# Fourier-domain channel mixing and MLP on one core: some DRAM stores issued from ScalarE's queue, with a reordered start of the second sequence

## The chip, the cores and the metric

The kernel runs on one core of a Trainium2 chip. The core has TensorE (PE, matrix multiply), VectorE (DVE), ScalarE (ACT), GpSimd (POOL) and SyncE (SP); in this kernel SP does nothing but issue DMA transfers. Each engine takes its own instructions in order. The metric is the device time of one execution in microseconds (us); less is better.

## The reference

The input x is 8 sequences of 3136 rows with 256 channels, in f32.

```
X  = rfft(x, axis=1)
Yr = Xr @ w_r - Xi @ w_i + b_r ;  Yi = Xr @ w_i + Xi @ w_r + b_i
Y  = soft-threshold(Yr, Yi, 0.01)
x1 = irfft(Y, n=3136)
u  = x1 + real(fft(fft(x1, axis=1), axis=2))
un = (u - mean(u)) / sqrt(var(u) + 1e-6)          # over the 256 channels
out = u + relu(un @ w_ch1) @ w_ch2                # 256 -> 1024 -> 256
```

The MLP weights arrive as 64-bit floats.

## The kernel before, in words

Each sequence goes through a chain of stages, each written as a Python generator. The transform over 3136 rows is split as 64 x 49.

- `p1` (for the first sequence, number 0, `p1_first`): loads x in chunks (`xf`), multiplies by the 64-point table (matmul L337 for sequence 0, L397 for sequence 1), copies the result out of PSUM into `ev` (ScalarE for even chunks, VectorE for odd ones), and stores `ev` into a DRAM scratch `a`. For sequence 0 that scratch lies in three parts: `a0` (frequencies 0 to 7), `a8` (8 to 15) and `ad` (16 to 31). The stores to `a0` go out first (L355). The stores to `a8` are gathered in a list `next8` (11), all others in a list `rest` (13). L362 issues `next8` and the first four of `rest` (15 in all), L367 the other nine.
- `p2_f2`: in four quarters q of eight frequencies each, two halves s per quarter, loads `af` (from `a`) and the table `tff` (L448, L450), and does the 49-point transform (matmul L468, 32 per quarter). The results are split into a high and a low part (`Xh`, `Xl`, `Xsh`, `Xsl`). The buffers `af` and `tff` are rings of three.
- `p2_w`: the complex channel product with the tables `wr`, `ws`, `wd`, three matmuls for one product (L154 to L156, tile `g_w`), then bias and soft threshold on VectorE (L534 to L537) into `Y`.
- `p2_mix`: the channel-axis transform of `Y`, put together in the tile `mq` on ScalarE, VectorE and GpSimd (L598 to L614), and stored to the DRAM scratch `md` (L619 to L633): ten stores for q = 0, six for each other quarter. `mq` is a ring of two.
- `p2_yt`, `p2_g2`: transposes of `Y` and the inverse 49-point transform, stored to `bd` (L696).
- `p3_norm`, `p3_tr`, `p3_mlp1`, `p3_mlp2`: the inverse 64-point transform (from `bd`, L720), the sum with `md` (loaded as `mt`, L740 and L742) into `ut` (L751), the statistics, and the two MLP products (tiles `h`, `o`).
- `weights`: loads the 64-bit MLP weights in eight pieces (`raw_w`, issued at L285; w1 in the buffers `W2` and `W3`, w2 in `Xh` and `Xl`, one buffer each) and splits each into a high and a low f32 part with six operations on VectorE (L179 to L189), two on ScalarE and two on GpSimd.

All f32 products but the simplest are three matmuls of split parts (`mm3`). The results in PSUM of all stages up to the MLP share four buffers (tag `g`).

The order of work is set in two steps. A heap takes the next step of the generator with the earliest due time (in units of T, the time slot of one sequence), which fixes the order in which instructions are written down; `after(...)` holds a generator back until another has passed a point. Then, when the program is built, each engine's instructions are ordered by readiness in a planned timeline, so that an instruction that is ready sooner can be put ahead of one written down earlier. `tc.issue_after(i)` keeps instructions of the same engine behind instruction i. Once built, the order on each engine is fixed. `behind(key, ...)` is a load on SP held behind an earlier load (key 3: the second `af` load of q = 1).

Before the change every DMA of the kernel is issued from SP (`st_eng = nc.sync`).

Of the kernel before, what the change touches and what calls it, by code (L numbers as in the profile page):

```python
# [132 lines left out]
def spectral_block(ctx: ExitStack, tc: tile.TileContext, x, w_ri, b_ri, w1, w2,  # L133
# [159 lines left out]
    def n2_rows(t, n0, n):  # L293

        return t[n0:n0 + n].rearrange("n c u d -> (c u) n d")
# [9 lines left out]
    def p1_first():  # L305


        a0 = dr.tile([N2, 2, 8, D], F32, tag="a0", bufs=1, name="a0")
        a8 = dr.tile([N2, 2, 8, D], F32, tag="a8", bufs=1, name="a8")
        ad = dr.tile([N2, 2, U - 16, D], F32, tag="ad0", bufs=1, name="ad0")  # L310
        ad1 = dr.tile([N2, 2, U, D], F32, tag="ad", bufs=4, name="ad1")
        a_dram[0] = lambda u: (a0, u) if u < 8 else (a8, u - 8) if u < 16 else (ad, u - 16)
        a_dram[1] = lambda u: (ad1, u)

        loads = [("xf", 2, 1)] * 2 + [("ut", UTB, 1)] * 2 + [("Y", 2, 3)] * 2 + [("Xh", 1, 2)]
        stores = [("uth", 2, 2), ("utl", 2, 2)] * 2 + [("W0", 1, 4)]
        slots = []
        for tag, bufs, z in loads:
            slots += [(tag, bufs, z, i) for i in range(z)]
        outs = []  # L320
        for tag, bufs, z in stores:
            outs += [(tag, bufs, z, i) for i in range(z)]
        slots.append(("Xl", 1, 1, 0))
        outs.append(("ev", 2, 1, 0))
        next8, rest = [], []
        todo = chunks + [(NM - 1, 1)]
        for ci, (m, n) in enumerate(todo):
            yield T * ci / len(todo)
            w = n * D
            tag, bufs, z, i = slots[ci]  # L330
            if i == 0:
                xf = sb.tile([128, z * 512], F32, tag=tag, bufs=bufs, name="xf")
                nn = z * 2 if n == 2 else 1
                for r, src in enumerate(x_rows(0, m, nn)):
                    af_ld["x"] = nc.sync.dma_start(out=xf[r * 64:r * 64 + 64, :nn * D], in_=src).ins
            g = gtile("g_f1")
            te.matmul(g[:, :w], fwd_0, xf[:, i * 512:i * 512 + w], start=True, stop=True)  # L337
            tag, bufs, z, i = outs[ci]
            if i == 0:
                ev = sb.tile([128, z * 512], F32, tag=tag, bufs=bufs, name="ev")  # L340
            (va.tensor_copy if ci % 2 else sc.copy)(ev[:, i * 512:i * 512 + w], g[:, :w])
            if i == z - 1:
                mb = m - 2 * i
                nn = m + n - mb
                for r in range(2):
                    v = ev[:, :nn * D].rearrange("p (n d) -> p n d", d=D)
                    if n == 1:
                        if r:

                            st_eng.dma_start(out=ad1[m:m + 1, :, 0:8].rearrange("n c u d -> c u (n d)"), in_=ev[16:32, :D])  # L350
                            rest.append((ad1[m:m + 1, :, 8:16].rearrange("n c u d -> c u (n d)"), ev[48:64, :D]))
                            rest.append((ad1[m:m + 1, :, 16:].rearrange("n c u d -> c u (n d)"), ev[96:128, :D]))
                            continue
                    n2 = NM * r + mb
                    st_eng.dma_start(out=n2_rows(a0, n2, nn), in_=v[r * 16:r * 16 + 16])  # L355
                    next8.append((n2_rows(a8, n2, nn), v[32 + r * 16:48 + r * 16]))
                    rest.append((n2_rows(ad, n2, nn), v[64 + r * 32:96 + r * 32]))
        done.add(("a0", 0))
        yield from after(("af", 1))
        for o, i in next8 + rest[:4]:  # L360
            with tc.issue_after(af_ld[1]):
                af_ld["rest"] = st_eng.dma_start(out=o, in_=i).ins  # L362
        done.add(("a8", 0))
        yield from after(("af", 3))
        for o, i in rest[4:]:
            with tc.issue_after(af_ld[3]):
                st_eng.dma_start(out=o, in_=i)  # L367
        done.add(("a", 0))

    def p1(b):  # L370
# [18 lines left out]
        for ci, (m, n) in enumerate(todo):  # L389
            yield T * (t0 + width * (ci - 1) / len(todo))  # L390
            load(ci)
            yield T * (t0 + width * ci / len(todo))
            w = n * D
            xf = xfs.pop(ci)
            g = gtile("g_f1")
            if b == 1:
                te.matmul(g[:, :w], fwd_f, xf[:, :w], start=True, stop=True)  # L397
            else:
                xh = sb.tile([128, 512], F32R, tag="xh", bufs=1, name="xh")
                xl = sb.tile([128, 512], F32R, tag="xl", bufs=1, name="xl")  # L400
                sc.copy(xh[:, :w], xf[:, :w])  # L401
                lo_g(xl[:, :w], xf[:, :w], xh[:, :w])
                mm3(g[:, :w], *K["fwd"], xh[:, :w], xl[:, :w])
            ev = sb.tile([128, 512], F32, tag="ev", bufs=2, name="ev")
            (va.tensor_copy if ci % 2 else sc.copy)(ev[:, :w], g[:, :w])
            for r in range(2):
                ad, n2 = (a_dram[b + r](0)[0], m) if n == 1 else (a_dram[b](0)[0], NM * r + m)
                st_eng.dma_start(out=n2_rows(ad, n2, n),
                                 in_=ev[r * 64:r * 64 + 64, :w].rearrange("p (n d) -> p n d", d=D))
        done.add(("a", b))  # L410

# [3 lines left out]
        t0 = T * (1.0, START1)[b] if b < 2 else T * (b + 2 - LEAD)  # L415
        return t0 + step * q, step, f2w, w0, ww, w0 + ww
    xt, yt_, tabs = {}, {}, {}
    w_mm, last_mm = {}, [None]

    def behind_w(b, on):  # L420

# [12 lines left out]
    def p2_f2(b):  # L434


        for q in range(4):
            base, STEP, F2W, W0, WW, M0 = clock2(b, q)
            u0 = 8 * q
            yield base  # L440
            yield from after((("a0", "a8")[q] if b == 0 and q < 2 else "a", b))
            xt[b, q] = Xh, Xl, Xsh, Xsl = x_tiles(b, q)
            afs, tfs = [], []
            for s in range(2):
                af = sb.tile([98, 4 * D], F32, tag="af", bufs=3, name="af")
                ad, u = a_dram[b](u0 + 4 * s)
                with tc.issue_after(af_ld["rest"]) if b == 0 and q == 1 else nullcontext():
                    ld = nc.sync.dma_start(out=af, in_=ad[:, :, u:u + 4].rearrange("n c u d -> (n c) (u d)"))  # L448
                tff = sb.tile([98, 4, 100], F32, tag="tff", bufs=3, name="tff")
                nc.sync.dma_start(out=tff, in_=c_tf[:, u0 + 4 * s:u0 + 4 * s + 4, :])  # L450
                afs.append(af)
                tfs.append(tff)
                if b == 0:
                    af_ld[2 * q + s] = ld.ins
                    done.add(("af", 2 * q + s))
            for ui in range(4):
# [6 lines left out]
                for s in range(2):  # L463
                    yield base + STEP * F2W * (ui / 4 + s / 8)
                    for k in range(2):
                        o = gv[:, k, :, s * S:s * S + S]
                        with behind_w(0, b == 0 and q == 1 and ui == 0):
                            te.matmul(o, afs[s][:, ui * D + k * 128:ui * D + k * 128 + 128], tfs[s][:, ui].rearrange("p (c j) -> p c j", c=2),  # L468
                                      start=True, stop=True)
                def put(f, outs, *ins):  # L470

                    both = len(outs[0]) == 1
# [70 lines left out]
    def p2_mix(b):  # L543
# [6 lines left out]
        def rows(d, first, nj, n):  # L550

            return d[first:first + 64 * nj].rearrange("(j k) d -> j k d", k=64)[:, 0:n]
# [3 lines left out]
        for q in range(4):  # L556
# [58 lines left out]
            mr = mq.rearrange("p a u h e -> p a (u h e)")  # L615
            mp, mm = (mq[:, i].rearrange("p u h e -> p u (h e)") for i in range(2))

            if q:
                st_eng.dma_start(out=rows2(u0, 24), in_=mr[0:24])  # L619
                st_eng.dma_start(out=rows2(u0 + 64 * 24, 1), in_=mr[24:25])  # L620
                st_eng.dma_start(out=rows2(61 - u0, 24), in_=mr[75:99])
            else:
                st_eng.dma_start(out=rows(mpd, 0, 25, 4), in_=mp[0:25])
                st_eng.dma_start(out=rows(mmd, 0, 25, 3), in_=mm[0:25, 1:4])
                st_eng.dma_start(out=rows(mpd, 61, 24, 3), in_=mp[75:99, 0:3])
                st_eng.dma_start(out=rows(mmd, 60, 24, 3), in_=mm[75:99, 0:3])

                st_eng.dma_start(out=rows(mmd, 63, 24, 1), in_=mm[1:25, 0:1])
                st_eng.dma_start(out=rows(mpd, 32, 24, 1), in_=mp[75:99, 3:4])
                st_eng.dma_start(out=rows(mmd, 31, 25, 1), in_=mm[75:100, 3:4])  # L630
            st_eng.dma_start(out=rows2(u0 + 4, 24), in_=mr[50:74])
            st_eng.dma_start(out=rows2(u0 + 4 + 64 * 24, 1), in_=mr[74:75])
            st_eng.dma_start(out=rows2(57 - u0, 24), in_=mr[25:49])  # L633
        done.add(("m", b))

    yhl = {}
# [278 lines left out]
```

## Time and profile before

| | us |
|---|---|
| three runs | 1932.55, 1924.45, 1930.68 |
| median | 1930.68 |
| profiled execution: its own time | 1925.76 |
| profiled execution: span, first to last instruction | 1923.5 |
| PE busy in the span | 1844.0 (96%) |
| DVE, ACT, POOL busy | 1259.7 (65%), 851.1 (44%), 701.5 (36%) |

The page of the profile cuts the span into 40 slices of 48 us. In the first four PE is busy 5, 7, 8 and 6 tenths, from then on nine tenths or more. The start, until the MLP of the first sequence runs, is thus where PE stands idle, and there the change lies. The span is the time between the first and the last instruction; the time of the execution has 2.3 us more around it.

### The profile page before, as it was taken

The page shows a single profiled execution, that of the slowest core. Times are in us where ns is not written, and L with a number is a line of the kernel's source. Part 1 is how long each engine was busy: PE and PEld are TensorE (multiplying, and loading weights), DVE is VectorE, ACT ScalarE, POOL GpSimd, SP SyncE. Part 2 cuts the span into 40 slices and gives each one's busy share as a digit, 9 for nine tenths or more (in the row PEclk, how much of TensorE's full clock was granted, in tenths as well). Part 3 has the DMA queues.
Part 4 walks back from the last instruction along what each step waited for, and adds up shares of the span by engine and source line. Part 5 has one row for each costly group of instructions (what it writes and reads, how often), then busy time and mean ns, then how long its engine had stood idle before and what let it go on. Part 6 is the DMA issues. An engine that isn't in the chain of part 4 may idle for free.

```text
span 1923.5 us, 34657 instructions
## 1 busy us (share of the span) xinstructions
PE 1844.0 (96%) x12123; PEld 1695.2 (88%) x12123; DVE 1259.7 (65%) x2726; ACT 851.1 (44%) x1892; POOL 701.5 (36%) x1093
## 2 busy tenths in 40 slices
PE   5786999999999999999999999999999999999999
PEld 3665999989999999989999999998999999998899
DVE  2886767767666766767666666765766776665443
ACT  2555545444544444444444544434454443433322
POOL 0455544333434334344323444323443332323110
PEclk7897999999999999999999999999999999999999
DMA  7666644354443545244443543435533343223110
GB/s 205 180 202 179 175 134 115 102 156 137 122 114 112 142 120 150 84 123 138 119 143 93 155 130 105 127 94 150 145 95 109 102 115 89 69 80 115 56 40 26
DMA packets 163715, 233.02 MB, mean 121 GB/s; under 512 B 27662, under 2 KB 107606, under 8 KB 163542
## 3 DMA queue, kind: packets, MB, share of 16 engines
q1 hardware_dynamic: 163542, 230.82, 42.5%
q8 instruction: 96, 1.57, 0.3%
q14 instruction: 77, 0.63, 0.1%
HBM read 127.95 MB, written 102.76 MB: 120 GB/s over the span
## 4 chain that ended last, share of the span: by engine, by line
PE 82%; DMA 6%; DVE 5%; SPq 3%; issue 1%; ACT 1%; POOL 1%; DVEq 0%; POOLq 0%; ACTq 0%
PE o L155 9%; PE o L154 9%; PE o L156 8%; PE h L154 8%; PE h L156 8%; PE h L155 8%; PE g_f L468 5%; PE g_w L154 3%; PE g_w L156 3%; PE g_w L155 3%; PE g_yt L663 2%; PE g_g L154 2%; PE g_g L155 2%; PE g_g L156 2%; PE g_ut L785 2%; DMA md<-mq 2%
## 5 line engine op out<-in xcount | busy, mean ns | idle before, releaser
L807 DVE SCALAR_TENSOR_TENSOR hl<-h,hh 128x512 fp32r<-128x512 f32 (+1 forms) x416 | 272.9, 656 | 332.7 <-ACT hh L806 330.8
L806 ACT ACTIVATE hh<-h 128x512 fp32r<-128x512 f32 (+1 forms) x416 | 238.5, 573 | 475.1 <-PE h L156 438.4
L155 PE MATMUL o<-w2h,hl 128*128 128x256 f32 x1568 | 429.0, 284 | 3.1 <-DVE hl L807 2.9
L156 PE MATMUL o<-w2h,hh 128*128 128x256 f32 x1568 | 422.7, 279 | 0.0
L154 PE MATMUL o<-w2l,hh 128*128 128x256 f32 x1568 | 391.3, 284 | 0.0
L154 PE MATMUL h<-utl,w1h 128*128 128x512 f32 (+1 forms) x832 | 323.9, 389 | 0.0
L156 PE MATMUL h<-uth,w1h 128*128 128x512 f32 (+1 forms) x832 | 317.7, 382 | 0.0
L155 PE MATMUL h<-uth,w1l 128*128 128x512 f32 (+1 forms) x832 | 317.5, 382 | 0.0
L155 PEld LDWEIGHTS o<-w2h,hl 128*128 128x128 f32 x1568 | 296.8, 189 | 9.3 <-DVE hl L807 4.2
L156 PEld LDWEIGHTS o<-w2h,hh 128*128 128x128 f32 x1568 | 296.4, 189 | 3.4
L154 PEld LDWEIGHTS o<-w2l,hh 128*128 128x128 f32 x1568 | 283.7, 189 | 12.5
L151 POOL TENSOR_TENSOR bl<-bf,bh 128x512 fp32r<-128x512 f32 x104 | 130.2, 1252 | 286.9 <-ACT bh L745 284.3
L156 PEld LDWEIGHTS h<-uth,w1h 128*128 128x128 f32 x832 | 156.3, 188 | 23.9
L151 POOL TENSOR_TENSOR xl<-xf,xh 128x512 fp32r<-128x512 f32 (+1 forms) x75 | 98.4, 1311 | 213.0 <-ACT xh L401 207.0
L154 PEld LDWEIGHTS h<-utl,w1h 128*128 128x128 f32 x832 | 156.6, 188 | 14.2 <-DVE hl L807 0.3
L155 PEld LDWEIGHTS h<-uth,w1l 128*128 128x128 f32 x832 | 156.7, 188 | 13.5
L468 PEld LDWEIGHTS g_f<-tff,af 98*128 98x128 f32 x1024 | 145.2, 199 | 24.3 <-issue 11.2
L468 PE MATMUL g_f<-tff,af 98*128 98x100 f32 x1024 | 151.9, 278 | 14.8 <-DMA tff<-c_tf 14.2
L151 POOL TENSOR_TENSOR Xl<-xx,Xh 128x400 fp32r<-128x400 f32 (+1 forms) x96 | 99.8, 1041 | 77.3 <-ACT Xh L482 39.7
L751 DVE TENSOR_TENSOR ut<-g_g,mt 128x512 f32<-128x512 f32 x104 | 68.2, 656 | 87.2 <-PE g_g L156 43.1
L151 POOL TENSOR_TENSOR Xsl<-xs,Xsh 128x200 fp32r<-128x200 f32 x120 | 75.5, 630 | 133.8 <-ACT Xsh L482 123.3
L760 POOL TENSOR_SCALAR vv<-ag 128x2 f32<-128x2 f32 x104 | 27.1, 260 | 208.8 <-DVE ag L757 185.2
(162 smaller groups left out, 3795.4 us busy)
## 6 DMA issues: line engine op xcount, KB each, us to landing
bd<-bev SPq DMA_DIRECT2D x128, 196.0 KB
bf<-bd SPq DMA_DIRECT2D x184, 128.0 KB
out_dram<-ut SPq DMA_DIRECT2D x92, 256.0 KB
af<-ad SPq DMA_DIRECT2D x60, 392.0 KB
xf<-in_x SPq DMA_DIRECT2D x176, 128.0 KB
ad<-ev SPq DMA_DIRECT2D x176, 128.0 KB
md<-mq SPq DMA_DIRECT2D x112, 192.0 KB
mt<-md SPq DMA_DIRECT2D x416, 32.0 KB
```

The lines of the kernel that those rows point to most:

```text
L151: gp.tensor_sub(out_, full, hi.bitcast(F32))
L154: te.matmul(o, lh, rl, start=start, stop=False)
L155: te.matmul(o, ll, rh, start=False, stop=False)
L156: return te.matmul(o, lh, rh, start=False, stop=stop)
L468: te.matmul(o, afs[s][:, ui * D + k * 128:ui * D + k * 128 + 128], tfs[s][:, ui].rearrange("p (c j) -> p c j", c=2), start=True, stop=True)
L663: te.transpose(gt[:100, (v * 2 + o) * 128:(v * 2 + o + 1) * 128], y[:, o, place].rearrange("p c j -> p (c j)"), ident)
L751: va.tensor_add(ut[:, :n], g[:, :w].rearrange("p (n d) -> p n d", d=D), mt[:, :n])
L760: gp.tensor_scalar(vv[:, :n], ag[:, :n, 1:2], 1.0, EPS, op0=ALU.mult, op1=ALU.add)
L785: te.transpose(gv[:, k, j * 128:(j + 1) * 128], ut[:, j, k * 128:(k + 1) * 128], ident)
L806: sc.activation(hh[:, :w], h[:, :w], AF.Relu)
L807: va.scalar_tensor_tensor(hl[:, :w], h[:, :w], 0.0, hh[:, :w].bitcast(F32), op0=ALU.max, op1=ALU.subtract)
```

## The change

Five things are changed, all of them in the first two sequences:

1. Of the 15 stores at L362 every second one (7), and of the nine at L367 every second one (4), is issued from ScalarE's queue (`nc.scalar`), without `issue_after`. SP keeps 8 and 5.
2. The first-stage matmuls of sequence 1 are written down only once `p2_f2` has written the second pair of frequencies of q = 1 of sequence 0, and the first of them is kept behind that matmul on PE (`f2_mm[0, 1, 1]`).
3. The first-stage stores of sequence 1 (L408, 24 of them) go out from ScalarE's queue for even chunks (12).
4. For sequence 0, q = 2, the loads of `af` and `tff` are due 0.1 T earlier and go into other buffers: one slot of the `mq` ring for both halves of `af`, the two slots of `eo` for `tff`.
5. All 28 `mq` stores of sequence 0 are issued from ScalarE's queue.

```diff
-        for o, i in next8 + rest[:4]:
+        for n, (o, i) in enumerate(next8 + rest[:4]):
+            if n % 2:
+                nc.scalar.dma_start(out=o, in_=i)
+                continue
             with tc.issue_after(af_ld[1]):
                 af_ld["rest"] = st_eng.dma_start(out=o, in_=i).ins
...
-        for o, i in rest[4:]:
+        for n, (o, i) in enumerate(rest[4:]):
+            if n % 2:
+                nc.scalar.dma_start(out=o, in_=i)
+                continue
             with tc.issue_after(af_ld[3]):
                 st_eng.dma_start(out=o, in_=i)
...
+            while b == 1 and (0, 1, 1) not in f2_mm:
+                yield now[0] + 10
...
             if b == 1:
-                te.matmul(g[:, :w], fwd_f, xf[:, :w], start=True, stop=True)
+                with tc.issue_after(f2_mm[0, 1, 1]) if ci == 0 else nullcontext():
+                    te.matmul(g[:, :w], fwd_f, xf[:, :w], start=True, stop=True)
...
-                st_eng.dma_start(out=n2_rows(ad, n2, n),
+                (nc.scalar if b == 1 and ci % 2 == 0 else st_eng).dma_start(out=n2_rows(ad, n2, n),
...
-    w_mm, last_mm = {}, [None]
+    w_mm, last_mm, f2_mm = {}, [None], {}
...
-            yield base
+            yield base - (0.1 * T if b == 0 and q == 2 else 0)
...
-                af = sb.tile([98, 4 * D], F32, tag="af", bufs=3, name="af")
+                roomy = b == 0 and q == 2
+                if roomy:
+                    if s == 0:
+                        wide = sb.tile([98, 8 * D], F32, tag="mq", bufs=2, name="af")
+                    af = wide[:, s * 4 * D:(s + 1) * 4 * D]
+                else:
+                    af = sb.tile([98, 4 * D], F32, tag="af", bufs=3, name="af")
...
-                tff = sb.tile([98, 4, 100], F32, tag="tff", bufs=3, name="tff")
+                tff = sb.tile([98, 4, 100], F32, tag="eo" if roomy else "tff", bufs=2 if roomy else 3, name="tff")
...
-                            te.matmul(o, afs[s][:, ui * D + k * 128:ui * D + k * 128 + 128], tfs[s][:, ui].rearrange("p (c j) -> p c j", c=2),
-                                      start=True, stop=True)
+                            f2_mm[b, q, ui] = te.matmul(o, afs[s][:, ui * D + k * 128:ui * D + k * 128 + 128], tfs[s][:, ui].rearrange("p (c j) -> p c j", c=2),
+                                      start=True, stop=True).ins
...
+            mix_eng = nc.scalar if b == 0 else st_eng
             if q:
-                st_eng.dma_start(out=rows2(u0, 24), in_=mr[0:24])
+                mix_eng.dma_start(out=rows2(u0, 24), in_=mr[0:24])
...
```

The other nine kinds of `mq` store are changed in the same way as the last one shown.

## Rows read from the trace of the kernel before

**Rows 1.** Busy time by stretch: the stretch in us from the span's start, its length, then the busy time of each engine with its instructions, the granted clock of TensorE as a share of full speed, the busy share of the 16 DMA engines, and GB/s.

```profile
26.00:46.00 20.00, 11.44 (x44) 10.74 (x44) 3.61 (x9) 5.30 (x15) 4.32 (x6) 0.51 0.87 232
46.00:62.00 16.00, 8.92 (x39) 7.81 (x40) 11.73 (x19) 4.73 (x9) 6.21 (x5) 0.68 0.79 230
62.00:85.00 23.00, 17.41 (x87) 12.75 (x85) 22.32 (x41) 13.13 (x38) 15.69 (x22) 0.93 0.53 147
85.00:117.00 32.00, 30.36 (x182) 25.88 (x180) 19.91 (x43) 19.67 (x53) 14.26 (x18) 1.00 0.66 188
117.00:157.00 40.00, 29.25 (x131) 22.85 (x131) 38.72 (x63) 20.05 (x46) 23.95 (x19) 0.83 0.70 210
157.00:200.00 43.00, 31.29 (x149) 26.53 (x149) 24.62 (x51) 21.47 (x48) 23.75 (x32) 0.80 0.61 168
...
200.00:400.00 200.00, 197.58 (x1342) 183.13 (x1340) 144.76 (x308) 98.72 (x223) 87.81 (x123) 1.00 0.46 128
```

**Rows 2.** Instructions of PE in order of time: start, duration, line, what; in brackets the idle time before and what ended it.

```profile
30.91 7.12 PE L468 MATMUL g_f<-tff,af 98*128 98x100 f32 x32 [9.64 <-DMA tff<-c_tf]
...
45.14 0.48 PE L156 MATMUL g_w<-Xh,wsh 128*128 128x400 f32 x1
53.08 2.04 PE L397 MATMUL g_f<-xf,fwd_f 128*128 128x512 f32 x2 [7.46 <-DMA xf<-in_x]
...
71.74 0.66 PE L468 MATMUL g_f<-tff,af 98*128 98x100 f32 x4 [3.15 <-DMA tff<-c_tf]
...
90.25 1.03 PE L468 MATMUL g_f<-tff,af 98*128 98x100 f32 x8
...
99.21 0.66 PE L468 MATMUL g_f<-tff,af 98*128 98x100 f32 x4 [1.40 <-DMA tff<-c_tf]
...
160.15 1.03 PE L468 MATMUL g_f<-tff,af 98*128 98x100 f32 x8
```

**Rows 3.** The chain of waits that ended last, from 36 to 64 us, in order of time: start, duration, what.

```profile
38.23 5.68 DMA tff<-c_tf
...
46.10 3.97 DMA raw_w<-in_w
...
50.10 0.43 DVE cv_w_ut L183
```

**Rows 4.** DMA issues of SP in order of time: start, duration of all together, line, what, count.

```profile
1.19 6.94 SPq L335 DMA_DIRECT2D xf<-in_x  x11
9.09 0.81 SPq L355 DMA_DIRECT2D a<-ev  x2
...
26.86 7.64 SPq L362 DMA_DIRECT2D a<-ev  x11
34.54 2.04 SPq L362 DMA_DIRECT2D ad<-ev  x4
...
38.66 7.38 SPq L367 DMA_DIRECT2D ad<-ev  x9
46.10 0.87 SPq L285 DMA_DIRECT2D raw_w<-in_w  x2
```

**Rows 5.** The DMA queue from 0 to 26 us: packets, MB, and the time that the packets took as a share of the 16 engines' time; under it two groups of store issues up to 70 us, with their count and the size of each.

```profile
q1 hardware_dynamic: 3655, 4.95, 74.6%
...
ad<-ev SPq DMA_DIRECT2D x14, 128.0 KB
...
a<-ev SPq DMA_DIRECT2D x16, 64.0 KB
```

**Rows 6.** The chain of waits around 119 us and from 165 to 185 us.

```profile
117.74 0.60 DVE ev L405
...
119.04 0.62 SPq L408
...
119.76 3.92 DMA raw_w<-in_w
...
168.03 0.17 DVE mq L613
...
169.47 0.60 SPq L408
...
170.84 0.49 SPq L619
...
173.58 3.88 DMA md<-mq
177.48 0.33 SPq L740
...
179.70 1.65 DMA mt<-md
```

**Rows 7.** Store issues on SP: line, what, count, and the shortest, median and longest duration in ns, with the first and last start (tile `mq` from 80 to 200 us; line L408 up to 220 us).

```profile
L408 SPq DMA_DIRECT2D ad<-ev x38: 574/620/1522, 55.8 to 219.4; - x38
...
L631 SPq DMA_DIRECT2D md<-mq x4: 305/374/378, 104.8 to 172.5; - x4
L632 SPq DMA_DIRECT2D md<-mq x4: 592/616/634, 105.1 to 172.9; - x4
...
L619 SPq DMA_DIRECT2D md<-mq x3: 303/317/491, 127.1 to 170.8; - x3
```

**Rows 8.** What SP's DMA queue waited for up to 220 us, of these stores alone: line and releaser, us in total, times, the longest.

```profile
SPq L624 <- DVE mq L613: 2.1, 1, 2.1
...
SPq L619 <- DVE mq L613: 1.6, 2, 0.9
...
SPq L623 <- POOL mq L610: 1.1, 1, 1.1
```

**Rows 9.** Instructions of ACT in order of time, as in rows 2.

```profile
13.87 0.59 ACT L341 COPY ev<-g_f 128x512 f32<-128x512 f32 x1 [4.12 <-PE g_f L337]
...
35.50 0.49 ACT L487 COPY xx<-g_f 128x400 f32<-128x400 f32 x1 [7.88 <-PE g_f L468]
...
105.65 0.38 ACT L598 COPY mq<-g_mix 100x256 f32<-100x256 f32 x1
```

**Rows 10.** The first-stage matmuls of sequence 1: line, what, count, shortest, median and longest duration in ns, first and last start in us.

```profile
L397 PE MATMUL g_f<-xf,fwd_f x24: 590/592/1190, 53.1 to 125.4; 128*128 128x512 f32 x24
```

More of the change, by code (lines that the diff above doesn't have):

```diff
@@ L616, in p2_mix @@
             mp, mm = (mq[:, i].rearrange("p u h e -> p u (h e)") for i in range(2))
+            mix_eng = nc.scalar if b == 0 else st_eng
             if q:
-                st_eng.dma_start(out=rows2(u0, 24), in_=mr[0:24])
-                st_eng.dma_start(out=rows2(u0 + 64 * 24, 1), in_=mr[24:25])
-                st_eng.dma_start(out=rows2(61 - u0, 24), in_=mr[75:99])
-            else:
[L623 to L633, printed above, removed]
+                mix_eng.dma_start(out=rows2(u0, 24), in_=mr[0:24])
+                mix_eng.dma_start(out=rows2(u0 + 64 * 24, 1), in_=mr[24:25])
+                mix_eng.dma_start(out=rows2(61 - u0, 24), in_=mr[75:99])
+            else:
+                mix_eng.dma_start(out=rows(mpd, 0, 25, 4), in_=mp[0:25])
+                mix_eng.dma_start(out=rows(mmd, 0, 25, 3), in_=mm[0:25, 1:4])
+                mix_eng.dma_start(out=rows(mpd, 61, 24, 3), in_=mp[75:99, 0:3])
+                mix_eng.dma_start(out=rows(mmd, 60, 24, 3), in_=mm[75:99, 0:3])
+                mix_eng.dma_start(out=rows(mmd, 63, 24, 1), in_=mm[1:25, 0:1])
+                mix_eng.dma_start(out=rows(mpd, 32, 24, 1), in_=mp[75:99, 3:4])
+                mix_eng.dma_start(out=rows(mmd, 31, 25, 1), in_=mm[75:100, 3:4])
+            mix_eng.dma_start(out=rows2(u0 + 4, 24), in_=mr[50:74])
+            mix_eng.dma_start(out=rows2(u0 + 4 + 64 * 24, 1), in_=mr[74:75])
+            mix_eng.dma_start(out=rows2(57 - u0, 24), in_=mr[25:49])
         done.add(("m", b))
```

## The prediction

> **What bounds the kernel now.** I read the page's slices first, then the busy time by stretch, then PE's instructions with the idle time ahead of each, then the chain of waits with SP's issues, and last ScalarE's instructions. From 200 us on PE is busy 197.58 of 200 us [rows 1]: whatever time the start saves is saved at the end, and nothing the change does later can matter. So the question is when the saturated part begins. In the start, from 26 to 200 us, PE is busy 128.7 of 174 us, and below 85 us it runs partly at its lower clock (granted 0.51 and 0.68, between the levels 1.2 and 2.4 GHz) [rows 1].
>
> Two stretches have VectorE as the bound instead: 62 to 85 us (22.32 of 23 busy) and 117 to 157 us (38.72 of 40) [rows 1]. Between them, at 85 to 117 us, PE is the bound (30.36 of 32). That matters for the reading of PE's idle time. The largest wait of PE inside the changed code is the 7.46 us ahead of the first-stage matmul of sequence 1 at 53.08, the next the 3.15 us at 71.74 and the 1.40 us at 99.21 for `tff` [rows 2]. But the chain of waits does not run through the 7.46 us. From 38 to 62 us it runs through the table load, SP's L367 stores, the `raw_w` load (46.10, 3.97 us), and VectorE's splitting of that weight from 50.10 on [rows 3]. A PE that gets on earlier finds VectorE busy with the weights. So only what makes `raw_w` land earlier counts in full there.
>
> **The change, part by part.**
>
> *Stores of the first stage on two queues.* SP spends 7.64 + 2.04 = 9.68 us on the 15 stores at L362 (0.645 each) and 7.38 on the nine at L367 (0.82 each), and then issues `raw_w` at 46.10 [rows 4]. It loses 7 of the first and 4 of the second: 7 x 0.645 + 4 x 0.82 = 7.8 us. That is the upper bound of how much earlier `raw_w` is issued. The lower bound is 0: the DMA engines are 0.87 busy from 26 to 46 us [rows 1], so the bytes may take their time whoever issues them. They have 0.13 x 20 = 2.6 us free there, and from 0 to 26 us 25.4% free, 6.6 us [rows 5]. The moved stores are not held by `issue_after`, and the build puts what is ready ahead (11 `xf` loads ahead of the first stores, though some are written behind them [rows 4]); ScalarE is idle 4.12 us before 13.87 and 7.88 before 35.50 [rows 9]. So I expect ScalarE to issue most of its 11 before 31 us, in free DMA time. Between 2.6 and 7.8 I take **5.0** us. VectorE's weight work then starts at 45 instead of 50.10.
>
> The same early stores compete with the `xf` loads of sequence 0, which hold the first `p2_f2` (PE idle 9.64 before 30.91 [rows 2]). Of the 11 about four, two of 64 and two of 128 KB, can be ready before 16 us; 384 KB at 190 GB/s (4.95 MB in 26 us) is 2.0 us [rows 5]. Bounds 0 and 2.0, taken **-1.0**, since not all of them need fall ahead of the last `xf` load.
>
> *First-stage matmul of sequence 1 behind `p2_f2` of q = 1.* PE's 7.46 us go: behind the last `ws` product at 45.14 comes `wd` at once. What is late next is VectorE, so I cost this at no gain of its own beside the 5.0. It is the cover for it: without it the 5.0 would be stopped by the same wait. The moved matmuls have room: the last starts at 125.4 [rows 10], and `p2_f2` of sequence 1 first reads their result at 160.15 [rows 2].
>
> *Loads of q = 2 early, in their own buffers.* The wait of 3.15 us goes; and since q = 2 no longer takes places in the rings of three, the second half of q = 3 needs not wait for one, which removes the 1.40 us. The 1.40 lie in the stretch where PE is the bound and count; the 3.15 lie in VectorE's full stretch, beside its work, and count little: bounds 1.4 and 4.55, taken **2.0**. The new holder of an `mq` slot delays nobody: `p2_f2` of q = 2 ends at about 91, and the next user of that slot, the mix of q = 1, starts at 105.65 [rows 2, 9].
>
> *Mix stores on ScalarE.* For the last quarter, VectorE's copy into `mq` is done at 168.2 and the first store issues on SP at 170.84, behind L408 and a `bd` load; the last `mq` store's landing releases the `mt` load at 177.48, and `mt` the first `ut` [rows 6]. On ScalarE the stores can go within half a microsecond of the copy. Bounds 0 and 2.6, taken **2.0**. The second part of the weights is not helped: its load at 119.76 stands behind an L408 store of a chunk that VectorE copied [rows 6], and odd chunks stay on SP.
>
> *What ScalarE pays.* No store is issued from ScalarE in this trace, so the price is bounded by SP's. 7.8 us for the first stage, 12 x 0.62 = 7.4 for L408, 28 x 0.436 (mean of the three medians 0.374, 0.616, 0.317) = 12.2 [rows 7]: 27.4 us in all. In addition a store waits on ScalarE for the others' part of `mq`, as it did on SP: 2.1 + 1.6 + 1.1 = 4.8 us [rows 8], with the PSUM copies of `g` buffers for the transposes, the inverse transform and `p2_f2` queued behind it, and PE behind these. ScalarE is busy 39.7 of 72 us between 85 and 157 [rows 1], so 32 us are free; 24 of the 51 stores fall there (mix of q = 0 and 1, and four chunks), 24 x 0.5 = 12 us. So most is hidden by idle time. Bounds 0 and 32.2, taken **-1.0** (nearest to the low end, as ScalarE stays at 72% busy).
>
> Sum: 5.0 - 1.0 + 2.0 + 2.0 - 1.0 = **7.0 us**. Against the profiled execution: 1925.8 - 7.0 = 1918.8. The median of the runs shown is 4.9 above that execution, so in their terms 1930.68 - 7.0 = **1923.7 us**.
>
> **The rivals.**
>
> *B, the split buys nothing.* The DMA engines are the limit until `raw_w` lands, or the build places ScalarE's stores late; the 5.0 is 0. For it: 0.87 busy from 26 to 46 us, 0.79 from 46 to 62 [rows 1]. Against it: a quarter of the engines' time free before 26 us [rows 5]. Then 2.0 us are left, 1928.7.
>
> By the Trainium skill, "DMA: Bandwidth & Descriptors", section "Issuing engines are not separate DMA queues", transfers from several engines run on the same 16 DMA engines and a second issuer saves only issue time; by that rule alone B would hold wherever the engines are full. The trace agrees as far as the share of 0.87 goes, and leaves the earlier free time open.
>
> *C, all upper bounds.* 7.8 + 4.55 + 2.6 = 15.0 us, 1915.7. For it: VectorE is idle 12 of 32 us between 85 and 117 [rows 1], so an earlier start could be carried on. Against it: two stretches full on VectorE.
>
> *D, ScalarE holds PE up; slower.* The stores block ScalarE where PE is the bound, 85 to 117 us and at the bursts of six to ten `mq` stores. It decides when more than 8 us (the gains less the 1.0) of the 32.2 reach PE. If an issue took the longest of L408, 1.52 us [rows 7], the 24 stores would take 36.5 us, more than the 32 free. With two thirds of 32.2 on PE, 21.5 - 8 = 13.5 us slower: 1944. Against it: four `g` buffers and an idle ScalarE between bursts.
>
> **How the numbers follow.** The forecast (gain 3 to 11 us, 1920 to 1928) has 0.48, B 0.22, C 0.20, D 0.10. A measurement of this kernel can tell about 0.5%, 9.7 us, from no change: faster means below 1921.0. That is C nearly whole (0.19) and the upper part of the forecast (0.15): 0.34. Slower means above 1940.3, most of D: 0.07. Within: 0.59. The range reaches from C's 1915.7 less the runs' scatter (4 us to either side) to B's 1928.7 and the mild part of D: 1912 to 1936.
>
> **What would show it.** Right: no wait of several us ahead of a first-stage matmul at about 53, `raw_w` issued near 41 and VectorE's first L183 near 45; no `tff` wait at 72 and 99; the six last `mq` stores issued within 1 us of VectorE's copy, and the first `mt` load some 8 us earlier than 177.5; PE full from about 193. Wrong: `raw_w` landing near 50 as before (B); idle PE released by ScalarE's copies (`yf`, `bev`, `xx`) between 85 and 160 (D); a first L468 later than 33.

## The result: 0.7% slower, with the start later than before

The changed kernel took 1942.47 us (median of seven runs, 1936.68 to 1945.45), the kernel before 1930.68 beside it. The ratio is 1.0072 [1.0057, 1.0088], so 11.8 us are lost where 7.0 were to be gained. The profiled execution of the changed kernel took 1936.68 us, 10.9 more than that of before; its span was 1934.6 us.

Busy time by stretch, changed kernel, with the columns of [rows 1]:

```profile
26.00:46.00 20.00, 7.12 (x32) 6.90 (x32) 6.10 (x12) 6.24 (x17) 4.33 (x6) 0.55 0.80 200
46.00:62.00 16.00, 10.96 (x39) 9.00 (x40) 11.31 (x18) 4.70 (x12) 5.55 (x6) 0.61 0.94 276
62.00:85.00 23.00, 16.42 (x81) 13.22 (x80) 21.97 (x38) 11.23 (x32) 15.67 (x22) 0.92 0.53 145
85.00:117.00 32.00, 27.80 (x147) 22.18 (x148) 17.21 (x39) 16.17 (x47) 8.25 (x12) 0.89 0.46 132
117.00:157.00 40.00, 31.86 (x153) 25.26 (x151) 32.44 (x54) 19.07 (x45) 22.91 (x20) 0.92 0.71 207
157.00:200.00 43.00, 25.48 (x115) 21.20 (x114) 23.51 (x42) 19.32 (x46) 21.77 (x18) 0.72 0.55 158
200.00:220.00 20.00, 17.28 (x107) 14.95 (x106) 16.96 (x39) 12.45 (x28) 12.99 (x25) 1.00 0.47 125
220.00:240.00 20.00, 20.00 (x139) 18.59 (x138) 15.01 (x30) 10.89 (x24) 8.58 (x14) 1.00 0.75 199
```

PE is full only from 220 us. Against [rows 1] its busy time falls by 4.3 us at 26 to 46, by 2.6 at 85 to 117, by 5.8 at 157 to 200 and by 2.7 at 200 to 220, where before it was full. It rises by 2.0 and 2.6 us at 46 to 62 and 117 to 157, and falls by 1.0 at 62 to 85. The sum is 11.8 us. Busy time hides part of the loss, since TensorE's clock differs too: from 85 to 117 us the granted clock was 0.89, between its levels of 1.2 and 2.4 GHz, instead of 1.00 (PE had waited 1.88 us ahead of 80.80 and 2.65 ahead of 85.69), and PE got through 147 matmuls instead of 182 in 27.80 us instead of 30.36. So everything is decided before 220 us, and in two places.

The first place is the very start. PE of the changed kernel in order of time, answering to [rows 2]:

```profile
23.11 2.39 PE L337 MATMUL g_f<-xf,fwd 128*128 128x512 f32 x6 [3.72 <-DMA xf<-in_x]
35.65 7.12 PE L483 MATMUL g_f<-tff,af 98*128 98x100 f32 x32 [10.15 <-DMA af<-a]
...
58.00 2.07 PE L406 MATMUL g_f<-xf,fwd_f 128*128 128x512 f32 x2 [3.32 <-DVE y L549]
...
115.10 2.07 PE L406 MATMUL g_f<-xf,fwd_f 128*128 128x512 f32 x2 [3.03 <-ACT bev L710]
...
174.22 1.09 PE L679 MATMUL g_yt<-ident,Y 128*100 128x128 f32 x4 [4.48 <-DVE mq L619]
...
193.68 0.70 PE L154 MATMUL g_w<-Xsl,wrh 128*128 128x400 f32 x1 [5.92 <-POOL Xsl L151]
```

The first matmul of `p2_f2` starts at 35.65 instead of 30.91, 4.74 us late, because the last matmuls of sequence 0's first stage waited for a load of `xf` until 23.11. SP issued that load late. These are SP's issues of `xf` behind its first eleven, in the kernel before, and then the same stretch of the changed kernel with the `a` stores that now stand between them:

```profile
9.94 1.11 SPq L335 DMA_DIRECT2D xf<-in_x  x2
...
12.62 2.16 SPq L335 DMA_DIRECT2D xf<-in_x  x2
...
16.31 0.47 SPq L335 DMA_DIRECT2D xf<-in_x  x1
```
```profile
9.68 0.47 SPq L335 DMA_DIRECT2D xf<-in_x  x1
12.69 3.58 SPq L355 DMA_DIRECT2D a<-ev  x4
16.66 0.47 SPq L335 DMA_DIRECT2D xf<-in_x  x1
18.47 0.77 SPq L355 DMA_DIRECT2D a<-ev  x2
19.29 1.87 SPq L335 DMA_DIRECT2D xf<-in_x  x3
```

The built order on SP has changed: four `a` stores, which wait for VectorE's copies into `ev` and for earlier DMAs to land, stand ahead of the second of these loads, and two more ahead of the last three. So the last three go out at 19.29 to 21.16 instead of by 16.78. The DMA queues from 0 to 26 us (columns of [rows 5]) show what has moved; `q10` is ScalarE's:

```profile
q1 hardware_dynamic: 3250, 4.63, 69.2%
q10 hardware_dynamic: 896, 0.79, 9.7%
...
ad<-ev ACTq DMA_DIRECT2D x4, 128.0 KB
...
a<-ev ACTq DMA_DIRECT2D x4, 64.0 KB
```

ScalarE issues eight stores, 0.79 MB, before the last `xf` load has landed. But their bytes aren't what holds that load: the two queues together take 78.9% of the engines' time, and the load issued at 19.29 releases PE at 23.11, 3.82 us later, while in the kernel before the load issued at 9.94 took 6.23 us to land. Why the build orders SP in this way when the stores are ScalarE's isn't shown.

The second place is ScalarE itself, behind each burst of `mq` stores. ScalarE at the first and the last burst, in order of time:

```profile
109.82 0.26 ACTq L640 DMA_DIRECT2D md<-mq  x1
...
112.54 0.65 ACTq L648 DMA_DIRECT2D md<-mq  x1
113.77 0.31 ACTq L649 DMA_DIRECT2D md<-mq  x1
114.12 0.45 ACT L497 CAST Xh<-xs 128x100 fp32r<-128x100 f32 x2 [6.04 <-DMA md<-mq]
114.47 0.58 ACT L710 COPY bev<-g_g 98x512 f32<-98x512 f32 x1
...
187.77 0.32 ACTq L635 DMA_DIRECT2D md<-mq  x1
...
191.44 1.11 ACTq L649 DMA_DIRECT2D md<-mq  x1
192.59 0.36 ACT L497 CAST Xsh<-xs 128x200 fp32r<-128x200 f32 x1 [4.30 <-DMA md<-mq]
```

Four such gaps lie ahead of ScalarE's copies: 6.04, 5.13 (at 142.24), 4.60 (at 173.60) and 4.30 us, 20.1 in all. Not all of this is issue: in the first, ScalarE waits 2.05 us, until 109.78, for VectorE's last copy into `mq` before the store of 109.82 can go. Three of them reach PE. At 114.47 ScalarE at last empties a PSUM buffer (`bev`), and PE, idle 3.03 us, goes on at 115.10. The 4.60 us hold the copy of `g_mix` into `mq`, that holds VectorE's L619 at 174.01 (idle 3.90), and that holds PE for 4.48 us until 174.22. The 4.30 us hold `Xsh`, and so GpSimd's `Xsl` at 193.02 (idle 3.31) and PE for 5.92 us until 193.68. That is 13.4 us of idle PE (not all of it lost time, as the experiments show); ahead of the same `Xsl` product PE waited 0.66 us before, at 170.61. The gap at 142.24, which six stores fill from 137.98 to 142.20 though the trace names VectorE as its releaser, holds a split of the MLP weights, and no PE wait stands right behind it.

The first `mt` load is issued at 195.73 instead of 177.48, the first `h` matmul runs at 209.69 instead of 194.03.

### The profile page after: what moved, and what is told of

Read it like the earlier page. It is cut to its first block, busy times and chain, and to the rows that moved or that the text cites. A ratio compares the mean times of both kernels' runs of the same rounds, so it can differ in the third digit from the quotient of the medians.

```text
span 1934.6 us, 34663 instructions
## 1 busy us (share of the span) xinstructions
PE 1844.8 (95%) x12123; PEld 1693.9 (88%) x12123; DVE 1259.9 (65%) x2726; ACT 849.0 (44%) x1892; POOL 700.6 (36%) x1093
## 4 chain that ended last, share of the span: by engine, by line
PE 81%; DMA 5%; DVE 4%; SPq 2%; ACT 2%; issue 1%; POOL 1%; ACTq 0%; DVEq 0%; POOLq 0%
PE o L155 9%; PE o L154 9%; PE o L156 8%; PE h L154 8%; PE h L156 8%; PE h L155 8%; PE g_f L483 4%; PE g_w L154 3%; PE g_w L156 3%; PE g_w L155 3%; PE g_yt L679 2%; PE g_g L154 2%; PE g_g L155 2%; PE g_g L156 2%; PE g_ut L801 2%; DMA md<-mq 2%
## 5 line engine op out<-in xcount | busy, mean ns | idle before, releaser
L552 POOL TENSOR_TENSOR Y<-y,m 128x400 f32<-128x400 f32 x56 | 63.6, 1137 | 106.0 <-DVE m L551 102.8
```

The source lines that it names most:

```text
L552: (va if b == 0 or o == 0 else gp).tensor_sub(y[:, o, :, c, :], y1, m)
```

## The experiments

In the expectations Q is the theory that ScalarE's queue costs the time (the early stores taken to be in the way of the `xf` loads, the bursts of `mq` stores in the way of ScalarE's copies), and R that the reordering does (items 2 and 4 of the change). Diffs are against the changed kernel unless said otherwise; ratios are to the kernel before, timed beside each, with 95% intervals. A trace shows one execution, and executions of one kernel differ: of `sp_first` 1922.93 to 1939.63 us, the profiled one being the slowest. Two traces of one program, those of `p1_only` and `p1_again` below, differ by 1.1 us at the first matmul of `p2_f2`, 1.7 at the first `mq` store and 2.9 at the first `h` matmul. So what traces of different kernels show at such points means little below 3 us; verdicts on time rest on the ratios, and the traces name the waits.

### Taking parts away

**All stores back on SP (`sp_all`)**, so that only the reordering is left:

```diff
-            if n % 2:
-                nc.scalar.dma_start(out=o, in_=i)
-                continue
...
-                (nc.scalar if b == 1 and ci % 2 == 0 else st_eng).dma_start(out=n2_rows(ad, n2, n),
+                st_eng.dma_start(out=n2_rows(ad, n2, n),
...
-            mix_eng = nc.scalar if b == 0 else st_eng
+            mix_eng = st_eng
```

> All stores back on SP; what is left of the change is the later first-stage matmul of sequence 1 and the early loads of q = 2. Theory Q (ScalarE's queue is what costs: its early stores hold up the xf loads, and its bursts of mq stores block its copies): no slower than the kernel before, 0 to 7 us faster, first 49-point matmul at 31 us as before. Theory R (the reordering of the two parts that are left costs): slower than before by 4 us or more.

Measured: 1924.45 us, 0.9982 [0.9969, 0.9996]. The reordering gains a little by itself, about 3.5 us; R falls. SP's issues of `xf` stand as before, and the first `p2_f2` starts at 30.08. Here the wait for `xf` has only moved to another place:

```profile
55.43 2.04 PE L400 MATMUL g_f<-xf,fwd_f 128*128 128x512 f32 x2 [7.86 <-DMA xf<-in_x]
```

**First-stage stores of sequence 0 back on SP (`sp_first`)**, the first part of that diff alone.

> Only the first stage's 24 late stores of sequence 0 back on SP, the rest as in the changed kernel. Q: the first 49-point matmul goes back from 35.7 to about 31 us, and the kernel stands 5 to 9 us above the one before instead of 11.8. R: still about 11 us above.

Measured: 1930.57, 1.0008 [0.9990, 1.0027]: these 11 stores account for 0.64% of the changed kernel's time. The first `p2_f2` is back at 31.14, as Q had it; the kernel stands 1.5 us above the one before, lower than the 5 to 9 expected.

**`mq` stores back on SP (`sp_mix`)**, the last part of that diff alone.

> Only the 28 mq stores of sequence 0 back on SP. Q: ScalarE's four blocks of 4.3 to 6.0 us are gone, PE starts its first 49-point matmul at 35.7 still, and the kernel stands 1 to 6 us above the one before. R: still about 11 us above.

Measured: 1931.78, 1.0027 [1.0012, 1.0042]: the 28 `mq` stores account for 0.45%. The time is within Q's 1 to 6 us, and the first `p2_f2` is still late, at 37.23.

**The 11 stores kept behind ScalarE's copies (`held_first`)**: still on ScalarE, but after the last first-stage copy of sequence 0.

```diff
+            last_copy = (va.tensor_copy if ci % 2 else sc.copy)(ev[:, i * 512:i * 512 + w], g[:, :w])
...
-                nc.scalar.dma_start(out=o, in_=i)
+                with tc.issue_after(last_copy.ins):
+                    nc.scalar.dma_start(out=o, in_=i)
```

> ScalarE keeps its 11 first-stage stores, but they are kept behind its last copy of the first stage, so none goes out before about 21 us. Q with the stores' early bytes as the cause: first 49-point matmul back near 31 us and 5 to 9 us above the kernel before. If the split onto two queues as such costs (whenever the stores go out): first matmul at 34 us or later and about 11 us above.

Measured: 1935.82, 1.0039 [1.0025, 1.0053]. About half of the price of these stores goes when they are held; the rest stays. SP's issues of `xf` are again in the order of the kernel before, and the first stage ends as early. ScalarE, and then PE:

```profile
28.22 5.85 ACTq L372 DMA_DIRECT2D ad<-ev  x4
34.11 0.40 ACT L234 CAST cs<-csf 128x256 fp32r<-128x256 f32 x1 [8.32 <-DMA ad<-ev]
```
```profile
33.25 3.07 PE L485 MATMUL g_f<-tff,af 98*128 98x100 f32 x13 [11.89 <-DMA tff<-c_tf]
```

The first `p2_f2` is now 2.3 us later than before instead of 4.7, so it isn't back near 31 as Q had it. That is little more than scatter: `mix_only` below has the order of `sp_all` up to 100 us on every engine and starts it at 32.16 instead of 30.08. Four store issues took ScalarE 5.85 us, and its next copy came after 8.32 us idle.

### Adding parts one by one to the reordering

**First-stage stores alone (`first_only`)**: `sp_all` with its first hunk undone.

> The two reorderings, and of the three moves to ScalarE's queue only the first stage's 11 stores of sequence 0. If their early bytes are the cause: first 49-point matmul at 35 to 37 us, and 4 to 7 us above the kernel before (8 to 10 above the kernel with all stores on SP). If they cost only beside the other two moves: within 2 us of the kernel with all stores on SP.

Measured: 1935.18, 1.0039 [1.0019, 1.0060], 0.57% above `sp_all`, so these stores cost without the other two moves, and as much. PE:

```profile
24.07 4.03 PE L337 MATMUL g_f<-xf,fwd 128*128 128x512 f32 x6 [3.70 <-DMA xf<-in_x]
38.06 2.21 PE L483 MATMUL g_f<-tff,af 98*128 98x100 f32 x9 [9.96 <-DMA af<-a]
```

SP's order is that of the changed kernel. The load that PE waits for until 24.07 is issued at 20.26 and lands in 3.67 us: late again, and not slow. The first `mq` store issues at 111.34 instead of 100.82 in `sp_all`. How the late start carries through to about 11 us in the end wasn't followed stage by stage.

**The L408 stores of even chunks alone (`p1_only`)**: `sp_all` with its second hunk undone. Timed once more later as **`p1_again`**.

> The two reorderings, and only the 12 first-stage stores of sequence 1 on ScalarE's queue. They come one pair at a time, behind a copy that ScalarE makes itself: expected within 3 us of the kernel with all stores on SP either way; above that by 4 us or more, single pairs block ScalarE too.

> The reorderings and only the 12 first-stage stores of sequence 1 on ScalarE's queue, timed again beside the one above, since the first timing rests on four runs: 0.4 to 0.9% faster than before if that timing holds; within 0.4% if it was chance.

Measured: 1916.33, 0.9933 [0.9911, 0.9955], and again 1918.30, 0.9943 [0.9924, 0.9963]. This part of the change is good, by some 0.4% beside `sp_all`, and with the reordering it beats both kernels; that is more than the 3 us expected. In the trace of `p1_again` the first `mq` store goes out at 96.27 (`sp_all`: 100.82), and the first `h` matmul starts at 188.59 (193.89). Some 2 us of this lead are there before the first moved store issues at 57.28, where both programs have the same order on every engine, so they are scatter.

**The `mq` stores alone (`mix_only`)**: `sp_all` with its third hunk undone.

> The two reorderings, and only the 28 mq stores on ScalarE's queue. If the bursts are the second cause: four waits of ScalarE of 3 to 6 us released by mq stores, and 4 to 7 us above the kernel with all stores on SP. If PE hides them: within 2 us of it.

Measured: 1935.66, 1.0036 [1.0022, 1.0050], 0.54% above `sp_all`, more than the 4 to 7 us expected. ScalarE's four gaps are 4.81, 3.34, 3.56 and 4.43 us, and its wait for VectorE's last copy ahead of the first burst is 0.47 us, so here the issues themselves fill the gap. ScalarE at the end of the first burst, and PE behind the first and the last:

```profile
104.83 0.67 ACTq L642 DMA_DIRECT2D md<-mq  x1
105.54 0.43 ACTq L643 DMA_DIRECT2D md<-mq  x1
106.02 0.58 ACT L704 COPY bev<-g_g 98x512 f32<-98x512 f32 x1 [4.81 <-DMA md<-mq]
```
```profile
106.66 2.08 PE L400 MATMUL g_f<-xf,fwd_f 128*128 128x512 f32 x2 [3.65 <-ACT bev L704]
...
187.03 0.70 PE L154 MATMUL g_w<-Xsl,wrh 128*128 128x400 f32 x1 [7.62 <-POOL Xsl L151]
```

In `sp_all` PE waits 1.36 us ahead of that `Xsl` product.

**Only the last quarter's six (`mix_q3`)**, the stores from which the prediction hoped for 2.0 us:

```diff
-            mix_eng = nc.scalar if b == 0 else st_eng
+            mix_eng = nc.scalar if b == 0 and q == 3 else st_eng
```

(on top of `sp_all`).

> The two reorderings, and only the last quarter's six mq stores on ScalarE's queue, the step from which I expected 2 us. If the step is right: the first mt load 2 us earlier than in the kernel with all stores on SP (177.6) and the time 1 to 3 us lower. If a store on ScalarE waits for landings as a burst does: first mt load at 177.6 or later and no gain.

Measured: 1924.75, 0.9988 [0.9972, 1.0005], not to be told from `sp_all`. ScalarE's last issue of the burst and the copy behind it:

```profile
174.06 1.59 ACTq L643 DMA_DIRECT2D md<-mq  x1
175.70 0.49 ACT L534 COPY ks<-g_w 128x400 f32<-128x400 f32 x1 [5.66 <-DMA md<-mq]
```

The burst starts 1.21 us earlier than in `sp_all` (169.74 against 170.95), but it takes 5.91 us where SP's took 3.15, and the first `mt` load comes at 178.73 against 177.58. Counted from the end of VectorE's last copy into `mq`, the first store issues 0.37 us behind it instead of 1.05, and the `mt` load 9.36 us instead of 7.68. No PE wait above 0.7 us lies between 170 and 179, so here the blocked ScalarE holds up no matmul: it costs where PE needs its next copy.

### Sizes and places

**Every second `mq` store (`p1_mix_half`)**: `p1_only`, and 14 of the 28 on ScalarE.

```diff
+            def mix_store(**kw):
+                turn[0] += 1
+                (nc.scalar if b == 0 and turn[0] % 2 == 0 else st_eng).dma_start(**kw)
```

> The reorderings, the first-stage stores of sequence 1 as in the change, and of the mq stores every second one on ScalarE's queue (14 of 28). If the price is the length of the block, it is about half: ScalarE's waits released by mq stores are 1.5 to 3 us each, and the kernel stands half way between the one without mq stores on ScalarE (0.67% faster than before) and the one with all (0.08% slower), 0.2 to 0.4% faster. If the price is that ScalarE waits for mq at all: as with all 28.

Measured: 1923.88, 0.9976 [0.9963, 0.9989], 0.38% above the mean of the two timings of `p1_only`: about half of the price of all 28 (`sp_first`: 0.70% above that mean), as the first expectation had it. ScalarE's two longest waits on these stores are 2.9 and 2.0 us.

**The `mq` stores spread out (`mix_spread`)**: `p1_only`, and the 22 stores of q = 0 to 2 on ScalarE, but two or three at a time, behind each of the next quarter's four `mq` copies; those of q = 3 on SP.

```diff
+                    cp_ = sc.copy(mq[:, 1, ui], gv[:, :, 0])
+                    for _ in range(-(-len(pend) // (4 - ui))):
+                        with tc.issue_after(cp_.ins):
+                            nc.scalar.dma_start(**pend.pop(0))
...
+                if b == 0 and q < 3:
+                    pend.append(kw)
+                else:
+                    st_eng.dma_start(**kw)
```

> The reorderings and the first-stage stores of sequence 1 as in the change; of the mq stores of sequence 0 those of q = 0 to 2 (22) on ScalarE's queue, but not in one burst: two or three behind each of the next quarter's four copies into mq; q = 3 on SP. If the length of a burst is what costs: no wait of ScalarE above 2 us released by mq stores, and within 0.2% of the kernel without mq stores on ScalarE. If their issue time as such costs, wherever it lies: about 22/28 of the loss seen with all 28 (0.75%), so 0.5 to 0.6% slower than that kernel.

Measured: 1917.66, 0.9943 [0.9922, 0.9964], the same as `p1_again`, timed beside it. ScalarE:

```profile
114.11 0.59 ACT L713 COPY bev<-g_g 98x512 f32<-98x512 f32 x1 [2.23 <-PE g_g L709]
114.50 0.68 ACTq L611 DMA_DIRECT2D md<-mq  x1
114.59 0.38 ACT L608 COPY mq<-g_mix 100x256 f32<-100x256 f32 x1
115.22 0.42 ACTq L611 DMA_DIRECT2D md<-mq  x1
```

The longest wait on an `mq` store is now 1.1 us. So 22 issues on ScalarE cost nothing that can be measured when copies stand between them: what costs is the burst. The spread stores also seldom wait for other engines' parts of `mq`, but that wait was only 0.47 us ahead of the first burst of `mix_only`, which cost 0.54% all the same. The run also sends the stores a quarter later and keeps the last quarter's on SP; `mix_q3` shows that the latter is worth nothing by itself.

**Some of the first stage's stores late (`rest_late`)**: `p1_only`, and four of the nine L367 stores on ScalarE behind its last `Xsh` copy of q = 0.

> The reorderings, the first-stage stores of sequence 1 as in the change, the mq stores on SP; of the first stage's stores of sequence 0 only four of the last nine on ScalarE, kept behind its last copy of the first 49-point quarter (about 44 us). If early bytes were the cause of the late start: first 49-point matmul at 30 to 31 us, raw_w issued 2 to 3 us earlier than 45.5, and as fast as without these four or up to 0.15% faster. If any first-stage store on ScalarE costs: slower than without them by 0.2% or more.

Measured: 1919.46, 0.9966 [0.9950, 0.9982]. The first `p2_f2` starts at 30.43, as it should without early stores, and `raw_w` is issued at 44.10 (45.49 in `p1_only`), but nothing is gained over `p1_only`: the ratio is 0.28% above the mean of its two timings, as the second expectation had it, though the intervals overlap. ScalarE still waits 5.6 us on `ad` stores ahead of a `ks` copy.

**All 24 L408 stores on ScalarE (`p1_all`)**: `p1_only` without `and ci % 2 == 0`.

> The reorderings, and all 24 first-stage stores of sequence 1 on ScalarE's queue, those of odd chunks too, whose copy VectorE makes. If what helps is SP's relief: 0.6 to 1.0% faster than before. If a store that waits for another engine's copy blocks ScalarE noticeably: slower than with the even ones alone (0.67% faster).

Measured: 1930.83, 1.0015 [1.0004, 1.0026], 0.8% worse than the even chunks alone, as the second expectation had it. Odd chunks are copied by VectorE. The largest wait of ScalarE on `ad` stores, 3.1 us ahead of an `Xh` copy, isn't behind a store of such a chunk, though: it follows a pair whose chunk ScalarE had copied itself at 63.45, and the pair took 2.70 us because the second store waited for an earlier `ad` store to land. PE behind it:

```profile
68.54 0.70 PE L154 MATMUL g_w<-Xl,wrh 128*128 128x400 f32 x1 [4.71 <-POOL Xl L151]
```

So whether the price is the wait for VectorE or the number of stores in flight stays open.

**Even chunks on the kernel before (`p1_before`)**: the kernel before, with item 3 of the change alone.

> The kernel before with one edit: the 12 first-stage stores of sequence 1 for even chunks on ScalarE's queue; no reordering. If these stores alone carry the gain of the kernel that has them and the two reorderings (0.67% faster): 0.4 to 0.7% faster than before. If they need the reorderings: within 0.2%.

Measured: 1928.90, 1.0007 [0.9993, 1.0021]: no gain without the reordering. In its profiled execution, the slowest of its ten, PE's wait for `xf` at 55.48 is 9.89 us (7.46 in [rows 2]); but that wait ends before the first moved store issues, so the move didn't make it.

## Why the prediction was wrong, point by point

Two moves that were to gain lost instead. The first-stage stores on ScalarE's queue, put at +5.0 - 1.0 us, cost 11 to 12 us (0.57% and 0.64%); the `mq` stores there, put at +2.0 and part of the -1.0 of ScalarE's price, cost 9 to 10 us (0.45% and 0.54%). The L408 stores gained some 8 us that weren't in the sum.

The parts add up roughly. Beside the kernel before: reordering -0.18%, L408 stores -0.44% (the mean of the two timings, less the reordering), first-stage stores +0.57%, `mq` stores +0.54%, together +0.49%; measured +0.72%. The 0.23% left, 4.4 us, is interaction of the parts and the scatter of the timings; it wasn't split further.

**Early stores against the `xf` loads, -1.0, bounds 0 to 2.0: failed, in size and in cause.** The step priced the stores' bytes at the rate of the engines, for four stores that were ready before 16 us. Five had been issued by then and eight by 19 us, and the first `p2_f2` came 4.74 us late, more than the upper bound. But the late load wasn't slow: SP issued it at 19.29, behind stores that wait. The step took SP's order as given, and the build had changed it. The sign "a first L468 later than 33" was met.

**The split, +5.0: failed, but only in part as in rival B.** SP's stretch from the first of these stores to `raw_w` fell from 19.24 us (26.86 to 46.10) to 11.39 (32.59 to 43.98), by 7.85 us, the step's upper bound of 7.8. But it began 5.73 us later, so `raw_w` was issued only 2.12 us earlier, and of these 1.89 were lost again before VectorE could start:

```profile
43.98 2.60 SPq L285 DMA_DIRECT2D raw_w<-in_w  x2
```
```profile
49.87 0.43 DVE L183 TENSOR_SCALAR cv_w_ut<-raw_w 128x512 int32<-128x512 int32 x1 [4.46 <-DMA raw_w<-in_w]
```

The two issues took 2.60 us (0.87 in [rows 4]), and VectorE began at 49.87 against 50.10 [rows 3]: 0.2 us for 5.0. The engines were 0.94 busy from 46 to 62 us (0.79 before), as in rival B; but most of the 7.85 us went with the late start, which B didn't have. By the Trainium skill, "DMA: Bandwidth & Descriptors", section "Issuing engines are not separate DMA queues", a second issuer saves issue time alone. The trace agrees: SP's stretch is 7.85 us shorter, and the load that follows it lands no faster. The 0.645 and 0.82 us per store of this step weren't issue time alone: in the kernel before SP waited 4.6 us in these 24 stores for loads of `af` and `tff` to land.

**The 7.46 us wait, at no gain of its own: right in the changed kernel.** It was replaced by 3.32 us for VectorE's `y` at 58.00, the engine that the prediction named as late next. But in `sp_all`, with the same two reorderings, a wait of 7.86 us for `xf` is still there. So its absence in the changed kernel, where PE is later, doesn't show that the reordering removes it.

**Early q = 2 loads, +2.0, bounds 1.4 to 4.55: right as far as is known.** Both `tff` waits are gone, and the reordering as a whole gained about 3.5 us in `sp_all`. The two reorderings weren't run apart, so which of them gained it isn't shown.

**`mq` stores on ScalarE, +2.0: no gain.** The step took issue on ScalarE to go at once behind the last copy and at SP's pace. In the changed kernel the first store does issue only some 0.8 us behind VectorE's last copy (185.81, 1.21 us long), but from there to the first `mt` load it takes 7.96 us, not 6.64 [rows 6]. `mix_q3` shows the same in isolation: counted from that copy, the start is 0.68 us earlier and the end 1.68 later, with no difference in time.

**ScalarE's price, -1.0, bounds 0 to 32.2: failed, with the start the main step to fail.** The `mq` stores alone cost 9 to 10 us. The step weighed the stores' summed issue time (12 us) against ScalarE's idle time (32 us) as if the one could be fitted into the other. But ScalarE issues a burst in order, and the copies behind it come after gaps of 4.30 to 6.04 us, whatever idle time lies elsewhere. Rival D had the mechanism, the bursts of six to ten `mq` stores named with it, and its 1944 us lies near the 1942.47. But D charged the issue times of all 51 stores and kept the gains of 8 us against them; here the L408 stores gained, and the start, which D did not name, gave about half of the loss. So its number came near by luck.

**What was not foreseen at all:** the L408 pairs of even chunks gain some 8 us with the reordering and nothing without it. The store follows ScalarE's own copy, so it waits for no other engine, two go at a time, and SP's queue need not wait at that place for ScalarE. Why this pays only behind the reordering is argued, not shown: the planned order on every engine shifts with each edit, and no run holds it fixed.

## What to carry to other kernels

A DMA issue moved to a computing engine costs by what stands behind it in that engine's order. As far as these runs go: move stores whose data that engine itself has just written, two or three at a time with copies between, not a burst of six to nine. Moving issues away from a queue can also change the built order of those that stay: read that order again, and look for loads that have fallen behind stores that wait. Sum issue times against idle time only where the idle time lies right there.

## What the runs showed of the hardware

Single issues on ScalarE take as long as on SP: the shortest issues 0.26 us, L417 0.59 to 0.77 us each for 12 (L408 on SP: 0.574 to 1.522 [rows 7]). A burst can take longer than its issues, with gaps between them: the six `mq` stores of the last quarter took 3.15 us on SP in `sp_all` and 5.91 us on ScalarE in `mix_q3`. As far as the chain of waits names what ends a gap, it is the landing of an earlier DMA. In the chain of waits of the changed kernel, the last store of the first burst issues when a store to `ad` lands, and that of the last burst when a store to `md` lands:

```profile
110.37 3.38 DMA ad<-ev
...
113.77 0.31 ACTq L649
```
```profile
188.13 3.27 DMA md<-mq
...
191.44 4.28 DMA md<-mq
```

The first of the two has nothing to do with `md`, so it isn't an order kept by the stores' destinations. On SP such waits hold up further issues alone; on ScalarE they hold up the copies. What ties an issue to an earlier DMA isn't shown.
